# Five steps of a small side computation moved out of the first chunk of a gated layer into the last expert blocks, and two first products taken in two column parts

## The chip, the cores and the metric

The kernel runs on one core of a Trainium2 chip. The metric is the device time of one execution in microseconds (us). TensorE (PE) multiplies matrices, VectorE (DVE), ScalarE (ACT) and GpSimd (POOL) work on elements, and SyncE (SP) issues most transfers, in the order of its program. Each engine runs its own list of instructions in order and waits at an instruction until what it needs is there.

## The reference, cut to what matters

```python
def reference(q, k, v, modality_id, w_gate, modality_bias, w1, w2, w_in, w_out):
    x = windowed_attention(q, k, v)                  # 2304 tokens x 512
    logits = x @ w_gate + modality_bias[modality_id]
    e_idx = argmax(logits); gate = max(softmax(logits))   # one of 8 experts for each token
    for e in range(8):                               # the expert layer
        m = e_idx == e
        y[m] = gate[m] * (relu(x[m] @ w1[e]) @ w2[e])     # 512 -> 1024 -> 512
    h = y @ w_in                                     # the gated layer, 512 -> 2048 -> 512
    g = where(h >= 1, h, where(h <= -1, 0, (h + 1) ** 2 / 4))
    return g @ w_out
```

## The kernel before, in words

All products are made of parts in TensorE's fp32r form: an operand is split into a high part `h` and a low part `l` (a cast on ACT, then a subtraction on DVE or POOL), and three products h·h, h·l, l·h are added up. The kernel has three stages.

1. **Attention and routing.** Tokens are sorted by expert, in blocks of 128.
2. **Experts.** The loop over `u` (1 to 9) works on pairs of blocks, `b = 2u-1` and `b + 1`. `up_unit(x, q)` makes a quarter of the hidden layer (24 matmuls of 256 columns; four quarters, `q` 0 to 3), `relu` evicts it, and `down_unit(hh, i)` makes one block's output (24 matmuls of 512 columns). `put_y` scales the output and stores it to `ys` in DRAM. Half of an expert's weights (four tiles of 512 KB) is loaded into `RA` by `load_halves` at the start of the up half, the other half into `raw` at its end. Near the end the unused conversion space is given up (`half_ends(12)`), and the gated layer's weight groups `WG<-wis` are loaded into it.
3. **The gated layer.** Tokens come in three chunks `c` of 768, weights in groups `g` of 256 columns. A `unit` makes one group by a scheme with seven products (A11, A12, S1 to S4, A22) in place of eight, from sums and differences of the token blocks (`sum_x`, lines 1196) that are then split (`split_x`, lines 1189 and 1190). The products are accumulated in `mx`, `mz`, `mv`, `mw`. `also(k)` runs between the products and holds everything else, written out by hand: transposes of gathered tokens (`turn_y`, `typ`), loads and splits of later weight groups (`group_load`, `group_steps`), and the rests. When the chunk is done a second layer (`ob`) follows.

**The rests.** Each expert has a few tokens that fill no block. They are worked in small products, one expert `n` at a time, in steps `(n, k)`: k = 0 and 1 are `rest_up` (eight matmuls of 256 columns with 32 rows of weights, `rhp`), k = 2 turns the hidden rows (`rtp`), k = 3 and 4 are `rest_down` (four matmuls of 512 columns, `ryp`), k = 5, for odd `n` only, adds into `rsum`. The weights that a step k = 0, 1, 3 or 4 reads are four tiles of 256 KB (`WR`); there is one set of them, so the load for the next step is issued when the step's own matmuls have been issued and read them. `rest_end()` runs a step 0, 1, 3 or 4 and gives back its load, `rest_mid()` a step 2 or 5; each does nothing when the next step is not of its kind. The list of steps:

```python
rsteps = [(n, k) for n in range(UR) for k in range(6 if n % 2 else 5)]   # UR = 5
```

Before the change one `rest_end` runs at the end of each half pair `b` from 7 to 17, the others in the first chunk, one after each unit; the last one, (4, 4), in chunk 1. All engines but POOL run in the order in which the code is written (`manual_schedule`), POOL too in the gated layer.

Of the kernel before, what the change touches and what calls it, by code (L numbers as in the profile page):

```python
# [23 lines left out]
D = 512  # L24
# [16 lines left out]
TH = 384  # L41
# [44 lines left out]
def moe_kernel(tc, qh, kh, vh, wgh, mod, mbias, wall, winh, wouth, out):  # L86
    nc = tc.nc
    with ExitStack() as ctx:
# [218 lines left out]
                    yield  # L307

        def scaled(y, yp, k):
            nc.scalar.activation(y[:, :D], yp, AF.Copy, scale=k[:, 0:1])  # L310
            nc.scalar.copy(y[:, D:], k)

        def put_y(b, yp, tile=None):
            y = tile if tile is not None else mp.tile([P, XW], F32, name="y", bufs=2)
# [71 lines left out]
        def relu(hh, q, hp):  # L386
            h, l = (a[q].rearrange("p a t -> p (a t)") for a in hh)
            nc.scalar.activation(h, hp, AF.Relu)  # L388
            nc.vector.scalar_tensor_tensor(out=l, in0=hp, scalar=0.0, in1=h, op0=ALU.max, op1=ALU.subtract)  # L389

        def down_unit(hh, i):
            yp = bank("yp")
            for f in range(8):
                h, l = (a[f // 2][:, f % 2, i * P:i * P + P] for a in hh)
                wh, wl = (w[4 + f // 2][:, f % 2 * 512:f % 2 * 512 + 512] for w in (WH, WL))
                nc.tensor.matmul(yp, h, wh, start=f == 0, stop=False)  # L396
                nc.tensor.matmul(yp, h, wl, start=False, stop=False)
                nc.tensor.matmul(yp, l, wh, start=False, stop=f == 7)
            return yp
# [757 lines left out]
                return lambda: rest_load(*q) if q else None  # L1157
            return lambda: None

        RB0 = 7  # L1160

        def rests(b):

# [112 lines left out]
        with tc.manual_schedule(engines=ORDERED):  # L1276
# [63 lines left out]
            for u in range(1, UU):  # L1340
                b = 2 * u - 1
                last = u == UU - 1
                load_halves(2 * u)
                if u > 1 and not last:
                    for i in range(2):
                        xlast = xg_tile(2 * u + 1 + i)
                        gather(2 * u + 1 + i, xlast)
                if u > 1:
                    hh = h_tiles()
                    for q in range(4):  # L1350
                        relu(hh, q, up_unit(x, q))
                        if q == 1:
                            split_half(u, (4, 5))
                            rest_mid()
                        if q < 2 and (b, q) != (CVE, 0):
                            early(b)
                        if q == 2:
                            stores()
                            for v in units[b + 1]:
                                conv0(v)  # L1360
                    split_half(u, (6, 7))
                else:
                    for v in units[b + 1]:
                        conv0(v)
                if u == 1:
                    tokens(5, 9)
                done = convert(units[b])
                if u == 2:
                    tokens(13, UB + 2)
                if b == 13:  # L1370
                    order(mp.tile([P, XW], F32, name="y", bufs=2))
                rests(b)
                half_ends(b)
                b += 1
                if u > 1:
                    load_halves(2 * u + 1)
                if last:
                    wide = [new_raw("wide") for _ in range(4)]
                    for i in range(3):
                        fetch(i, wide[i][:, 0:XW])  # L1380
                if u == 1:
                    put_y(b - 1, down_unit(hh, 0))
                if not last:
                    for i in range(2):
                        turn_x(2 * u + 1 + i, x, i, new_gk())
                    split_half(u + 1, range(4))
                if u > 1:
                    put_y(b - 1, down_unit(hh, 0))
                    rest_mid()
                    early(b)  # L1390
                if last:
                    fetch(3, wide[3][:, 0:XW])
                    for i in range(3):
                        turn_y(i, ygs[i])
                    for o in ("A11", "A12"):
                        split_x(o)
                stores()
                for v in units[b + 1]:
                    conv0(v)
                if u == 1:  # L1400
                    tokens(9, 13)
                    idc = mp.tile([P, NE, NT], F32, name="idc")
                    nc.scalar.copy(idc, ids_ps)
                    mask = rest_tables()
                if u == 2:
                    rests_b(val, mask)
                put_y(b, down_unit(hh, 1))
                done = convert(units[b])
                if not last:
                    early(b)  # L1410
                    rests(b)
                half_ends(b)
                if u == UU - 2:
                    xgs, xs_u = {UB % 2: xg1, (UB + 1) % 2: xlast}, [gk[UB - 2], gk[UB - 1]]
                    yt = mp.tile([P, XW], F32, name="y", bufs=2)
                    gt = [new_gk() for i in range(2)]
                    more(UU)
# [12 lines left out]
                cfree.append(cfree[0])  # L1430
                return cfree.pop(0)

            def prod(o, s, out, first):
                h, l = (w[:, PROD[o]].rearrange("p (k w) -> p k w", k=2) for w in group_parts(None, s))
                xh, xl = sx[o]

                mms = [(w[:, k], xh[:, k]) for k in range(2) for w in (h, l)] + [(h[:, k], xl[:, k]) for k in range(2)]
                for n, (a, b) in enumerate(mms):
                    nc.tensor.matmul(out, a, b, start=first and n == 0, stop=n == 5, skip_group_check=not first)  # L1439

            def put_g(c, f, h, src):

# [17 lines left out]
            def unit(c, g, s, opened, also):  # L1460

                x, c1 = opened or open_x(s)
                also(0)
                z, v = bank("mz", (P, TH)), bank("mv", (P, TH))
                prod("S2", s, z, True)
                c2 = new_c()
                nc.vector.tensor_add(c2, z, c1)
                also(1)
                prod("S1", s, v, True)
                c5 = new_c()  # L1470
                nc.scalar.copy(c5, v)  # L1471
                also(2)
                if not opened:
                    close_x(c, g, s, x)
                also(3)
                prod("S3", s, z, False)
                nc.vector.tensor_add(c1, z, c1)
                also(4)
                prod("S4", s, v, False)
                nc.vector.tensor_add(c2, v, c2)  # L1480
                put_g(c, 2 * g, 1, c2)
                nc.vector.tensor_add(c5, c1, c5)  # L1482
                put_g(c, 2 * g + 1, 1, c5)
                also(5)
                w = bank("mw", (P, TH))
                prod("A22", s, w, True)
                nc.vector.tensor_add(c1, w, c1)
                put_g(c, 2 * g + 1, 0, c1)
                also(6)
# [83 lines left out]
            with tc.manual_schedule(engines=ORDERED | {E.Pool}):  # L1573
# [3 lines left out]
                for c in range(NCH):  # L1577
                    opened = {}
                    if c == 0:

                        for i in range(3):
                            opened[i] = open_x(ORD[0][i][1])
                            if i:
                                close_x(c, *ORD[0][i - 1], opened[i - 1][0])
                        turn_y(3, ygs[3])
                        close_x(c, *ORD[0][2], opened[2][0])
                        rest_mid()
                        load = rest_end()
                        turn_y(4, ygs[4])
                        for part, t in (((0, 256), 4), ((256, TH), 5)):  # L1590
                            if t > 4:
                                turn_y(t, ygs[t])
                            for i in range(2):
                                sum_x(i, nc.vector, part)
                            for o in ("S2", "S1"):
                                split_x(o, part)
                    for i, (g, s) in enumerate(ORD[c]):
                        last = i == NG - 1

                        def also(k):  # L1600
# [4 lines left out]
                                if k in (1, 2, 3):  # L1605
                                    split_x(("S3", "S4", "A22")[k - 1])
                            if c == 0:
                                if k == 3:
                                    rest_mid()
                                if k == 6 and i:  # L1610
                                    rest_end()()
                                if (i, k) == (0, 3):
                                    load()
                                for g, at in ((3, (0, 0)), (4, (0, 6)), (5, (1, 6)), (6, (2, 6))):
                                    if (i, k) == at:
                                        group_load(g, g)
                                if steps_at(1, 4, i, k):
                                    next(lg_)
# [140 lines left out]
```

## Time and profile before

| | |
|---|---|
| time, median of 3 runs | 808.7 us (808.5 to 810.07) |
| the profiled execution: its time | 812.92 us |
| its span in the trace | 811.2 us |
| TensorE busy in the span | 764.3 us, 94% |
| VectorE, ScalarE, GpSimd busy | 506.3, 349.5, 299.5 us |

The span is that of one profiled execution, from its first instruction to its last; the median is that of unprofiled runs. TensorE is busy nearly all the time; matmuls are pipelined, so a busy TensorE is not one at its peak.

### The profile page before, as it was taken

The page shows a single profiled execution, that of the slowest core. Times are in us where ns is not written, and L with a number is a line of the kernel's source. Part 1 is how long each engine was busy: PE and PEld are TensorE (multiplying, and loading weights), DVE is VectorE, ACT ScalarE, POOL GpSimd, SP SyncE. Part 2 cuts the span into 40 slices and gives each one's busy share as a digit, 9 for nine tenths or more (in the row PEclk, how much of TensorE's full clock was granted, in tenths as well). Part 3 has the DMA queues.
Part 4 walks back from the last instruction along what each step waited for, and adds up shares of the span by engine and source line. Part 5 has one row for each costly group of instructions (what it writes and reads, how often), then busy time and mean ns, then how long its engine had stood idle before and what let it go on. Part 6 is the DMA issues. An engine that isn't in the chain of part 4 may idle for free. (4 is left out here: it accounts for less than half of the span.)

```text
span 811.2 us, 14415 instructions
## 1 busy us (share of the span) xinstructions
PE 764.3 (94%) x4893; PEld 658.9 (81%) x4893; DVE 506.3 (62%) x1012; ACT 349.5 (43%) x827; POOL 299.5 (37%) x257
## 2 busy tenths in 40 slices
PE   7999779999999999898989888999999999999996
PEld 6888668999887887687778767999987788888884
DVE  6788888797775647412745644898878456553540
ACT  5899644233233226315333423343455435443340
POOL 5000562223332244111632321333744556475441
PEclk9999979999999999989899999999999999999999
DMA  9888942447797869234675554557855453343411
GB/s 206 232 232 251 290 122 50 147 169 253 244 329 256 285 224 375 87 117 151 204 245 167 182 205 149 188 186 230 271 207 149 121 150 116 105 130 102 138 53 39
DMA packets 101014, 149.21 MB, mean 184 GB/s; under 512 B 30096, under 2 KB 65456, under 8 KB 100928
## 3 DMA queue, kind: packets, MB, share of 16 engines
q1 hardware_dynamic: 95664, 132.30, 51.8%
q0 software_dynamic: 4736, 15.61, 6.1%
q8 instruction: 41, 0.67, 0.4%
q10 hardware_dynamic: 528, 0.26, 0.1%
q14 instruction: 45, 0.37, 0.1%
HBM read 132.00 MB, written 45.50 MB: 219 GB/s over the span
## 5 line engine op out<-in xcount | busy, mean ns | idle before, releaser
L1571 POOL TENSOR_TENSOR AR<-RA,AR 128x768 fp32r<-128x768 f32 x43 | 81.8, 1923 | 44.3 <-ACT AR L1570 44.2
L1683 PE MATMUL ob<-WG,AR 128*128 128x512 f32 x234 | 92.1, 394 | 1.2 <-POOL AR L1571 1.0
L82 POOL TENSOR_TENSOR cv_g<-cv_g,cv_a 128x512 f32<-128x512 f32 x32 | 45.2, 1426 | 129.5 <-DVE cv_a L80 98.2
L1681 PE MATMUL ob<-WG,AR 128*128 128x512 f32 x234 | 91.6, 391 | 0.0
L1682 PE MATMUL ob<-WG,AR 128*128 128x512 f32 x234 | 91.2, 390 | 0.0
L380 PE MATMUL hp<-xh,AR 128*128 128x256 f32 x512 | 73.5, 286 | 3.3 <-ACTq L1310 3.3
L380 PEld LDWEIGHTS hp<-xh,AR 128*128 128x128 f32 x512 | 66.6, 193 | 7.0 <-ACTq L1310 3.8
L1562 DVE TENSOR_SCALAR small<-RA 128x768 f32<-128x768 f32 x48 | 44.8, 935 | 36.7 <-DMA RA<-gs 36.7
L1563 ACT ACTIVATE small<-small,half 128x768 f32<-128x768 f32 x48 | 44.9, 937 | 41.5 <-DVE small L1562 41.5
L475 ACT ACTIVATE ex<-sm,nm 128x128 f32<-128x128 f32 x144 | 56.1, 394 | 15.2 <-DVE nm L468 14.8
L1439 PE MATMUL mz<-AR,WG 128*128 128x384 f32 x252 | 55.6, 357 | 6.7 <-ACT AR L1189 3.7
L1569 DVE TENSOR_TENSOR RA<-small,RA 128x768 f32<-128x768 f32 x48 | 56.0, 1167 | 6.3 <-ACT small L1563 5.2
L389 DVE SCALAR_TENSOR_TENSOR hl<-hp,hh 128x512 fp32r<-128x512 f32 x32 | 21.8, 689 | 53.9 <-ACT hh L388 33.5
L1439 PE MATMUL mv<-AR,WG 128*128 128x384 f32 x252 | 53.6, 347 | 1.5 <-ACT wide L1471 1.4
L1439 PEld LDWEIGHTS mz<-AR,WG 128*128 128x128 f32 x252 | 46.7, 199 | 9.8 <-ACT AR L1189 4.0
L1683 PEld LDWEIGHTS ob<-WG,AR 128*128 128x128 f32 x234 | 43.9, 188 | 13.2 <-POOL AR L1571 3.9
L1439 PE MATMUL mx<-AR,WG 128*128 128x384 f32 x252 | 52.5, 347 | 1.8 <-ACT small L1450 1.5
L1570 ACT CAST AR<-RA 128x768 fp32r<-128x768 f32 x48 | 39.9, 831 | 32.6 <-DVE RA L1569 15.8
L463 PE MATMUL sc<-K,qz 128*128 128x128 f32 x288 | 45.6, 309 | 8.3 <-DMA K<-in_kh_dram 5.0
L396 PE MATMUL yp<-AR,hh 128*128 128x512 f32 x128 | 51.6, 403 | 0.8 <-ACTq L351 0.8
L1439 PEld LDWEIGHTS mx<-AR,WG 128*128 128x128 f32 x252 | 45.2, 193 | 8.3 <-issue 6.4
L1682 PEld LDWEIGHTS ob<-WG,AR 128*128 128x128 f32 x234 | 43.9, 188 | 9.5
(395 smaller groups left out, 1734.4 us busy)
## 6 DMA issues: line engine op xcount, KB each, us to landing
WR<-in_wall_dram SPq DMA_DIRECT2D x80, 256.0 KB
RA<-in_wall_dram SPq DMA_DIRECT2D x36, 512.0 KB
raw<-in_wall_dram SPq DMA_DIRECT2D x36, 512.0 KB
RA<-gs SPq DMA_DIRECT2D x48, 384.0 KB
gs<-small SPq DMA_DIRECT2D x51, 192.0 KB
cv_r<-in_winh_dram SPq DMA_DIRECT2D x16, 512.0 KB
gs<-wide SPq DMA_DIRECT2D x36, 192.0 KB
V<-in_vh_dram SPq DMA_DIRECT2D x7, 768.0 KB
```

Of the source, the lines that this page charges most:

```text
L82: nc.gpsimd.tensor_add(z, z, x)
L380: nc.tensor.matmul(o, a, c, start=n == 0, stop=n == 11)
L396: nc.tensor.matmul(yp, h, wh, start=f == 0, stop=False)
L463: nc.tensor.matmul(sc[:, hp], Q[:, gi % 3, hp].rearrange("p a b -> p (a b)"), K[:, hp, s * 64:s * 64 + 128], start=True, stop=True)
L475: nc.scalar.activation(ex[:, hp], sm[:, hp], AF.Exp, bias=nm[:, hp:hp + 1], scale=1.0, accum_out=su[:, hp:hp + 1])
L1439: nc.tensor.matmul(out, a, b, start=first and n == 0, stop=n == 5, skip_group_check=not first)
L1563: nc.scalar.activation(GQ[n % 4], GQ[n % 4], AF.Square, scale=0.5, bias=half[:, 0:1])
L1569: nc.vector.tensor_max(GT[n % 5], GQ[n % 4], GT[n % 5])
L1571: eng.tensor_sub(l, GT[n % 5], h)
L1681: nc.tensor.matmul(obs[i], h[:, sl], wh, start=f == j == 0, stop=False)
L1682: nc.tensor.matmul(obs[i], h[:, sl], wl, start=False, stop=False)
L1683: nc.tensor.matmul(obs[i], l[:, sl], wh, start=False, stop=f == 7 and j == 1)
```

## The change

- In blocks 13 to 16 (`RX`) `rest_end` and `rest_mid` are called more often: after quarters 0, 1 and 2 of an up half, in the middle and at the end of the first `down_unit`. Nine steps, (1, 3) to (3, 1), run in these four blocks where four ran, and block 17 runs (3, 2) and (3, 3): (2, 4), (3, 0), (3, 1), (3, 2) and (3, 3) leave the gated layer. Chunk 0 keeps (3, 4), ahead of its units, and (3, 5) to (4, 3). The load for (4, 0) goes out in unit 3 in place of unit 4.
- In chunk 0 the transposes of the sixth token tile (`turn_y(5)`) are issued ahead of the splits of the first 256 columns, and unit 0's first products S2 and S1 are taken in two parts, 256 and 128 columns: S2 and S1 of the first part, then S2 and S1 of the second.
- `scaled` copies the gate columns ahead of the output, not behind it.

```diff
         def scaled(y, yp, k):
+            nc.scalar.copy(y[:, D:], k)
             nc.scalar.activation(y[:, :D], yp, AF.Copy, scale=k[:, 0:1])
-            nc.scalar.copy(y[:, D:], k)
...
-        def down_unit(hh, i):
+        def down_unit(hh, i, between=None):
             yp = bank("yp")
             for f in range(8):
+                if f == 4 and between:
+                    between()
...
-        RB0 = 7
+
+        RB0, RX = 7, (13, 14, 15, 16)
...
                         relu(hh, q, up_unit(x, q))
+                        if b in RX and q == 0:
+                            rest_mid()
                         if q == 1:
                             split_half(u, (4, 5))
+                            if b in RX:
+                                rest_end()()
+                            else:
+                                rest_mid()
+                        if b in RX and q == 2:
                             rest_mid()
...
-                    put_y(b - 1, down_unit(hh, 0))
-                    rest_mid()
+                    if b in RX:
+                        put_y(b - 1, down_unit(hh, 0, rest_mid))
+                        rest_end()()
+                    else:
+                        put_y(b - 1, down_unit(hh, 0))
+                        rest_mid()
...
-                put_y(b, down_unit(hh, 1))
+                if b in RX:
+                    put_y(b, down_unit(hh, 1, rest_mid))
+                else:
+                    put_y(b, down_unit(hh, 1))
...
-                prod("S2", s, z, True)
+                if (c, g) == (0, 0):
+                    prod("S2", s, z, True, PARTS[0])
+                    prod("S1", s, v, True, PARTS[0])
+                    prod("S2", s, z, False, PARTS[1])
+                else:
+                    prod("S2", s, z, True)
...
-                prod("S1", s, v, True)
+                if (c, g) == (0, 0):
+                    prod("S1", s, v, False, PARTS[1])
+                else:
+                    prod("S1", s, v, True)
...
-                        for part, t in (((0, 256), 4), ((256, TH), 5)):
-                            if t > 4:
-                                turn_y(t, ygs[t])
-                            for i in range(2):
-                                sum_x(i, nc.vector, part)
+                        for i in range(2):
+                            sum_x(i, nc.vector, PARTS[0])
+                        turn_y(5, ygs[5])
+                        for part in PARTS:
+                            if part[0]:
+                                for i in range(2):
+                                    sum_x(i, nc.vector, part)
                             for o in ("S2", "S1"):
                                 split_x(o, part)
...
-                                if k == 3:
+                                if k == 3 and i >= 4:
                                     rest_mid()
-                                if k == 6 and i:
+                                if k == 6 and i >= 5:
                                     rest_end()()
-                                if (i, k) == (0, 3):
+                                if (i, k) == (3, 3):
                                     load()
```

On TensorE, in the up half of block 13, the second to the fourth quarter and what follows stood so before (`hp` are the quarters, `rtp` and `ryp` are rest steps (1, 2) and (1, 3), `xp` the transposes of the next pair's tokens):

```order
L1087 MATMUL rtp<-ident,rh 128x128 x2
L380 MATMUL hp<-xh,AR 128x256 x8
L380 MATMUL hp<-xl,AR 128x256 x4
L380 MATMUL hp<-xh,AR 128x256 x8
L380 MATMUL hp<-xl,AR 128x256 x4
L380 MATMUL hp<-xh,AR 128x256 x8
L380 MATMUL hp<-xl,AR 128x256 x4
L380 MATMUL hp<-xh,AR 128x256 x8
L380 MATMUL hp<-xl,AR 128x256 x4
L351 UNCONDITIONAL_BRANCH
L1095 MATMUL ryp<-WR,rht 32x512 x4
```

After the change the same place has step (1, 3) after the second quarter and (1, 4) after the fourth:

```order
L1097 MATMUL ryp<-WR,rht 32x512
L351 UNCONDITIONAL_BRANCH
L1097 MATMUL ryp<-WR,rht 32x512 x3
L380 MATMUL hp<-xh,AR 128x256 x8
L380 MATMUL hp<-xl,AR 128x256 x4
L380 MATMUL hp<-xh,AR 128x256 x8
L380 MATMUL hp<-xl,AR 128x256 x4
L380 MATMUL hp<-xh,AR 128x256 x8
L380 MATMUL hp<-xl,AR 128x256 x4
L380 MATMUL hp<-xh,AR 128x256 x8
L380 MATMUL hp<-xl,AR 128x256 x4
L351 UNCONDITIONAL_BRANCH
```

The two rest steps of `down` now stand half an up half apart, where one stood; `L1097 MATMUL ryp<-WR,rht 32x512 x4`, step (1, 4), is the next row.

On SP this stood before the change behind the load for step (1, 4), of which the first row is the last of four tiles (`ISA` rows work out addresses; `er_i` and `on_i` are reads of registers):

```order
L1071 DMA WR<-in_wall_dram 128x512
L1225 DMA WG<-wis 128x1024
L1305 TENSOR_LOAD on_i
L1305 ISA x2
L241 ISA
L241 DMA raw<-in_wall_dram 128x1024
```

and this after it:

```order
L1073 DMA WR<-in_wall_dram 128x512
L1069 TENSOR_LOAD er_i
L1069 ISA x2
L1073 ISA
L1073 DMA WR<-in_wall_dram 128x512
L1073 ISA
L1073 DMA WR<-in_wall_dram 128x512
L1073 ISA
L1073 DMA WR<-in_wall_dram 128x512
L1073 ISA
L1073 DMA WR<-in_wall_dram 128x512
```

The load for (2, 0) now stands ahead of `WG<-wis` and `raw`. What stands ahead of the load for (1, 4) is as before: the load for (1, 3), the first `WG<-wis`, three register reads, four loads into `RA`.

On SP in chunk 0, around the load of the group that unit 7 works on (`WG<-wis`), there stood before:

```order
L1443 DMA gs<-small 128x384
L1067 TENSOR_LOAD er_i
L1067 ISA x2
L1071 ISA
L1071 DMA WR<-in_wall_dram 128x512
L1071 ISA
L1071 DMA WR<-in_wall_dram 128x512
L1071 ISA
L1071 DMA WR<-in_wall_dram 128x512
L1071 ISA
L1071 DMA WR<-in_wall_dram 128x512
L1225 DMA WG<-wis 128x1024
```

and now:

```order
L1464 DMA gs<-small 128x384 x3
L1464 DMA gs<-wide 128x384 x3
L1464 DMA gs<-small 128x384
L1228 DMA WG<-wis 128x1024
L1464 DMA gs<-small 128x384
```

The four loads `WR` for step (4, 0) no longer stand ahead of that `WG<-wis`; they stand seven stores (`gs`) earlier.

## Rows read from the trace of the kernel before

**Rows 1.** Page, part 1: busy us (share of the span) and instructions.

```profile
PE 764.3 (94%) x4893; PEld 658.9 (81%) x4893; DVE 506.3 (62%) x1012; ACT 349.5 (43%) x827; POOL 299.5 (37%) x257
```

**Rows 2.** Timeline of PE, blocks 13 to 16: start, us, instructions [idle before, releaser].

```profile
293.67 1.19 PE L380 MATMUL hp<-xh,AR 128*128 128x256 f32 x8
...
299.50 1.06 PE L1095 MATMUL ryp<-WR,rht 128*32 128x512 f32 x8
...
305.15 0.49 PE L396 MATMUL yp<-AR,hh 128*128 128x512 f32 x1 [0.77 <-ACTq L351]
...
314.36 1.06 PE L1095 MATMUL ryp<-WR,rht 128*32 128x512 f32 x8
...
327.70 1.07 PE L1080 MATMUL rhp<-WR,xst 128*32 128x256 f32 x16
...
340.93 1.07 PE L1080 MATMUL rhp<-WR,xst 128*32 128x256 f32 x16
```

**Rows 3.** Timeline of SP's queue, same blocks: when each load was issued.

```profile
288.35 3.10 SPq L1071 DMA_DIRECT2D WR<-in_wall_dram  x4
297.94 0.33 SPq L1225 DMA_DIRECT2D WG<-wis  x1
300.36 2.22 SPq L241 DMA_DIRECT2D RA<-in_wall_dram  x4
302.85 2.28 SPq L1071 DMA_DIRECT2D WR<-in_wall_dram  x4
```

**Rows 4.** Two stretches: busy time by engine, PE clock, DMA share, GB/s.

```profile
298.00:306.00 8.00, 6.88 (x43) 4.71 (x42) 2.81 (x6) 2.61 (x6) 2.14 (x2) 1.00 0.78 253
306.00:310.00 4.00, 4.00 (x17) 3.29 (x18) 3.56 (x9) 4.00 (x6) 0.70 (x2) 1.00 1.04 393
```

**Rows 5.** Timeline of PE in chunk 0, units 2 to 6.

```profile
408.21 1.06 PE L1080 MATMUL rhp<-WR,xst 128*32 128x256 f32 x12
411.59 0.63 PE L1080 MATMUL rhp<-WR,xst 128*32 128x256 f32 x4 [2.33 <-DMA WR<-in_wall_dram]
...
416.95 1.21 PE L1439 MATMUL mx<-AR,WG 128*128 128x384 f32 x6
...
421.90 1.06 PE L1095 MATMUL ryp<-WR,rht 128*32 128x512 f32 x8
...
426.15 1.20 PE L1439 MATMUL mx<-AR 128*128 128x384 f32 x6
...
429.72 1.21 PE L1439 MATMUL mw<-AR 128*128 128x384 f32 x6
...
440.67 1.79 PE L1080 MATMUL rhp<-WR,xst 128*32 128x256 f32 x16
...
447.31 1.32 PE L1439 MATMUL mx<-AR,WG 128*128 128x384 f32 x6 [1.52 <-ACT small L1450]
...
454.32 1.21 PE L1439 MATMUL mw<-AR,WG 128*128 128x384 f32 x6
```

**Rows 6.** Timeline of SP's queue in chunk 0.

```profile
403.19 2.06 SPq L1071 DMA_DIRECT2D WR<-in_wall_dram  x4
...
435.66 3.59 SPq L1071 DMA_DIRECT2D WR<-in_wall_dram  x4
439.30 0.43 SPq L1225 DMA_DIRECT2D WG<-wis  x1
```

**Rows 7.** Timeline of DVE in chunk 0: the first step on unit 7's weight group.

```profile
444.61 0.42 DVE L1234 TENSOR_TENSOR small<-WG 128x256 f32<-128x256 f32 x1 [5.81 <-DMA WG<-wis]
```

**Rows 8.** Timeline of all engines at unit 0's first products (S2 in mz, S1 in mv).

```profile
386.64 3.78 POOL L1196 TENSOR_TENSOR RA<-RA 128x768 f32<-128x768 f32 x2 [7.25 <-DVE RA L1196]
387.03 3.67 DVE L1190 TENSOR_TENSOR AR<-RA,AR 128x256 fp32r<-128x256 f32 x2 [0.47 <-ACT AR L1189]
387.05 2.75 PE L1439 MATMUL mz<-AR,WG 128*128 128x384 f32 x6 [3.74 <-ACT AR L1189]
...
391.56 1.46 PE L1439 MATMUL mz<-AR,WG 128*128 128x384 f32 x6
```

More of the change, by code (lines that the diff above doesn't have):

```diff
@@ L1431, in new_c, with prod @@
                 return cfree.pop(0)
-            def prod(o, s, out, first):
+            PARTS = ((0, 256), (256, TH))
+            def prod(o, s, out, first, part=ALLT):
                 h, l = (w[:, PROD[o]].rearrange("p (k w) -> p k w", k=2) for w in group_parts(None, s))
-                xh, xl = sx[o]
+                xh, xl = (x[:, :, part[0]:part[1]] for x in sx[o])
+                out = out[:, part[0]:part[1]]
                 mms = [(w[:, k], xh[:, k]) for k in range(2) for w in (h, l)] + [(h[:, k], xl[:, k]) for k in range(2)]
                 for n, (a, b) in enumerate(mms):
-                    nc.tensor.matmul(out, a, b, start=first and n == 0, stop=n == 5, skip_group_check=not first)
+                    nc.tensor.matmul(out, a, b, start=first and n == 0, stop=n == 5, skip_group_check=not first or part is not ALLT)
             def put_g(c, f, h, src):
```

## The prediction

> **What bounds the kernel now.** I read the page first: TensorE (PE) is busy for 94% of the span [rows 1], so time is won or lost where PE waits, or where it runs slowly behind a wait. Then I followed PE's timeline through the two stretches that the change touches, and at each wait the row of the queue that it waited for.
>
> In the expert blocks PE hardly waits. From the rest step at 299.50 us to the next at 314.36 it takes 14.86 us; the same work two blocks on, from 327.70 to 340.93, takes 13.23 [rows 2]. The excess of 1.63 lies at 305.15, where PE waits for ScalarE. In chunk 0 it waits more. Rest step (3, 1) starts at 408.21 and stops for 2.33 us for the last of its four weight tiles, issued from 403.19 on [rows 5, 6]. Around the change of unit at 440.67 there are waits again, for an evicted copy that ScalarE makes late [rows 5]. The row to see there is VectorE's: it had stood for 5.81 us, until 444.61, for the weights of unit 7 [rows 7], which SP had issued at 439.30, behind the four tiles of step (4, 0) [rows 6]; ScalarE's casts of these weights stand ahead of its evictions. The first stop of chunk 0 is 3.74 us at 387.05, for the split of S2 [rows 8].
>
> **What moving the steps costs in the expert blocks.** The steps' own work (some 1.0 us each, as the rows of 1.06 and 1.07 show, less the overlap with the next row) is the same on both sides: (2, 4), (3, 0), (3, 1), (3, 3) at 1.0 and two transposes, 4.1 us, leave chunk 0 and come in here. PE is full in both places, so it sums to nothing. What matters is that each step needs a load of four tiles (1.05 MB) that can start only when the step before is done, and that the steps now stand half an up or a down apart, 5.8 us (293.67 to 299.50 [rows 2]), where about 13 us lay between them.
>
> *Step (1, 3)* comes at 293.67 in place of 299.50. Its load was issued from 288.35 on [rows 3]. How long such a load takes, from its first issue to its last tile, the trace shows once: 403.19 to 411.59, 8.4 us, with other loads around it [rows 5, 6]. From below: issue 2.3 us, and 1.05 MB at 393 GB/s [rows 4] 2.7 us, together 5.0. So it lands between 293.4 and 296.8; the last tile is wanted at 294.4. A wait of 0 to 2.4 us; I take 1.4.
>
> *Step (1, 4)* is the dear one. Its load is issued right behind (1, 3), but on SP's queue it stands behind the first `WG<-wis` (0.5 MB), which went out only at 297.94 (the space that it fills is given up then), three register reads, and four loads into RA (2.1 MB) from 300.36 on; so it goes out from 302.85 on [rows 3], in the changed kernel as before, since nothing ahead of it has moved. PE is at the step at 293.67 + 1.0 + 1.4 + 5.8 = 301.9, before the load is even issued. When does it land? From 297.94 on 3.67 MB have to come in. At 253 GB/s until 306.00 and 393 after [rows 4] 2.02 MB are in by 306.00 and 3.59 by 310.00: the last tile lands at 310.2, and the step ends at 310.5. Without any wait it would end at 293.67 + 1.0 + 5.8 + 1.0 = 301.5. So **the two steps cost 9.0 us together**. From below: RA and this load, 3.15 MB, at 393 GB/s from 300.36 on, end at 308.4, 7.2 us. From above: 8.4 us from 302.85 on, 10.0 us. The Trainium skill, DMA: Bandwidth & Descriptors, section Queues, rings and completion order, says that descriptors of one issuing engine's queue are consumed in ring order on each DMA engine. No row here shows in which order the bytes of the two loads came; by that rule the tiles come after RA, as I summed, and without it the load could be in at 302.85 + 5.0 = 307.9 and the cost would be 6.7.
>
> *Behind the wait* PE's matmuls run slowly for a while. After the 2.33 us at (3, 1) that is measured: 408.21 to 416.95 is 8.74 us, and the same run of step, mx, mz, mv in a calm unit, 421.90 to 426.15, 4.25 [rows 5]. Of the 4.49 us lost 2.33 are the wait; **2.2 us** are the slow matmuls. I take that here too; the bounds are 0 and, the wait being much longer, 4.4.
>
> *Given back*: the excess of 1.63 us at 305.15 goes. ScalarE is ready at 305.2, when PE still stands at step (1, 4). **-1.6.**
>
> *The later steps* (2, 1), (2, 3), (2, 4) and (3, 1) have the step before them 5.8 + 1.0 = 6.8 us earlier. With a load time of 5.0 to 8.4 us the wait is 0 to 1.6 us each. I take **0.6** for all four, 6.4 as the upper bound. (2, 0) and (3, 0) stand a whole down and the transposes behind, and wait for nothing; (3, 3) has an up half.
>
> Sum here: 9.0 + 2.2 - 1.6 + 0.6 = **+10.2 us**.
>
> **What it gives in chunk 0.** Step (3, 1) is gone with its load: **-4.5** (the 4.49 above). Behind it unit 3 needs weight group 3, whose splits wait for nothing of the rests, so no other wait takes the place.
>
> Unit 7's weight group no longer stands behind the four tiles: SP can issue it behind the store of unit 4, at some 435.7 in place of 439.30 [rows 6], and the load has the queue to itself. It was in 5.3 us after its issue (439.30 to 444.61 [rows 6, 7]); it would be there by 441.0 at the latest, and by 439.4 at the bandwidth bound, where VectorE was ready at 444.61 - 5.81 = 438.8. So ScalarE's casts come 3.6 to 5.2 us earlier, and the evicted copy on which PE waited is in time. Step (4, 0) has its tiles too, since they are loaded a unit earlier. What PE loses there: 440.67 to 454.32 is 13.65 us, and the same run (step, mx, mz, mv, mx, mz, transposes, mv) in a calm unit, 421.90 to 429.72, 7.82 [rows 5]. **-5.8.** From below nothing, if the weights still come late.
>
> **The first products in two parts.** PE can begin S2 on 256 columns some 3 us earlier, but the end is set by the second part. VectorE's two subtractions for it took 3.67 us, from 387.03 to 390.70; GpSimd's two sums ran from 386.64 to 390.42 [rows 8]. VectorE's sums and subtractions of both parts stand in the same order as before, only the transposes move, so the last one will end at 390.7 again. What is left for PE then is two matmuls of 128 columns where it was two of 384: of the 0.86 us from 390.70 to 391.56 about two thirds go, **-0.6**. The twelve matmuls more lie in PE's wait; without that cover they would cost at most what twelve of 384 columns do, 2.4 us (six take 1.20 [rows 5]). The skill's page SBUF — State Buffer, section Who interferes with whom, says that a VectorE instruction with two SBUF inputs and a reading GpSimd instruction exclude each other for a whole instruction, and the first to start wins; [rows 8] agree, since a subtraction of 1.8 us comes out at half of GpSimd's time. By it the sum is the 0.6 above; without that lock the two subtractions would end by 388 and the gain would be near 3. `scaled` moves 0.2 us of ScalarE's work that nothing waits for: nothing.
>
> Sum: -4.5 - 5.8 - 0.6 = **-10.9 us**. Net 10.2 - 10.9 = **-0.7**. The profiled execution took 812.92 us, the median of the runs is 808.7, 0.5% less; a difference of this size is the same on either: 812.2 and **808.0 us**. A measurement of this kernel can tell 0.2%, 1.6 us, from no change. So I forecast no change that can be told: two large terms that nearly cancel.
>
> **Rivals.**
> *The later loads are late as well (slower).* Place: steps (2, 1) to (3, 1), four distances of 6.8 us. It decides once a load takes more than 6.8 us from its first issue. For it: the one load that the trace times took 8.4. Against: at the rate of [rows 4] a load that comes alone takes 5.0. At 1.6 each it is +5.8 on the forecast: 813.8.
> *The wait at (1, 4) is short and PE is not slowed behind it (faster).* 7.2 in place of 9.0, and 0 in place of 2.2: 804.0. For it: less competes with the load, since the next group and `raw` now stand behind it. Against: 3.15 MB don't come in faster than [rows 4] show.
> *VectorE gets its second part in ahead of GpSimd (faster).* Everything of the first unit moves up by 2.4 more: 805.6. Against: GpSimd waits for the same sum and needs no cast first.
> *The change doesn't do what it says in unit 5 (slower or the same).* Unit 7's group is late for another reason, as the stores ahead of it on SP wait for VectorE: only the slow step (4, 0), 0.7 of 5.8, is won: 813.1.
>
> **How the numbers follow.** Forecast 0.50, with its own range 805.5 to 810.0; the late loads 0.17; the short wait 0.15; VectorE first 0.08; unit 5 unmended 0.10. Of the forecast's half, 0.32 lie within 1.6 us of 808.7, 0.15 below, 0.03 above. Faster: 0.15 + 0.15 + 0.08 = 0.38; the same 0.32; slower: 0.03 + 0.17 + 0.10 = 0.30. The range leaves out the late loads and reaches from the short wait to unit 5: 803.5 to 813.2.
>
> **What the profile after would show.** Right: in block 13 a wait of PE for `WR` of 7 to 9 us ahead of the second `ryp`, slow matmuls behind it, and the end of block 16 some 14 us later than before; no wait at unit 2 or around unit 5 in chunk 0; S2 in two parts, the second ending with VectorE near GpSimd's second sum. Wrong: no such wait in block 13 (the change would be faster by some 10 us), or waits for `WR` at three or more of the later steps (slower), or unit 5 as before.

## The result, and the profile after

| | before | after |
|---|---|---|
| time, median of 9 runs each | 808.7 us (803.35 to 816.12) | 817.52 us (812.27 to 820.36) |
| the profiled execution: its time | 812.92 us | 817.52 us |
| its span | 811.2 us | 815.8 us |

The ratio of the runs is 1.0113, with an interval from 1.0081 to 1.0145: the change makes the kernel slower by 9 us, outside the range of the prediction. A second series of runs gave the same ratio (below). The two profiled executions differ by only 4.6 us, and that is what their rows can explain. The page of the changed kernel answers to [rows 1]:

```profile
span 815.8 us, 14439 instructions
PE 765.0 (94%) x4905; PEld 657.3 (81%) x4905; DVE 508.8 (62%) x1012; ACT 350.6 (43%) x827; POOL 300.8 (37%) x257
```

TensorE is busy as long as before, 765.0 us against 764.3; what is longer is its waiting. Its timeline in blocks 13 to 17 answers to [rows 2]:

```profile
286.74 1.07 PE L1082 MATMUL rhp<-WR,xst 128*32 128x256 f32 x16
293.80 3.52 PE L1097 MATMUL ryp<-WR,rht 128*32 128x512 f32 x8
...
309.39 3.83 PE L1097 MATMUL ryp<-WR,rht 128*32 128x512 f32 x8 [6.22 <-DMA WR<-in_wall_dram]
313.15 1.63 PE L293 MATMUL xp<-ident,xg 128*128 128x128 f32 x8
...
321.16 1.07 PE L1082 MATMUL rhp<-WR,xst 128*32 128x256 f32 x16
...
328.31 0.63 PE L1082 MATMUL rhp<-WR,xst 128*32 128x256 f32 x4 [0.28 <-DMA WR<-in_wall_dram]
...
329.62 1.26 PE L1082 MATMUL rhp<-WR,xst 128*32 128x256 f32 x12 [0.68 <-DMA WR<-in_wall_dram]
...
336.87 1.06 PE L1097 MATMUL ryp<-WR,rht 128*32 128x512 f32 x8
343.72 1.20 PE L1097 MATMUL ryp<-WR,rht 128*32 128x512 f32 x8
...
363.44 2.04 PE L380 MATMUL hp<-xh,AR 128*128 128x256 f32 x8 [3.88 <-PEq L1313]
```

Step (1, 3) at 293.80 takes 3.52 us where 1.06 is its work: its four tiles came one after another, the last weight load for it at 296.27. Step (1, 4) begins after a wait of 6.22 us, at 309.39, and takes 3.83. Step (2, 1) at 328.31 waits twice for a tile, 0.28 and 0.68. The last row, the first of block 17, stood in the kernel before at

```profile
345.34 2.07 PE L380 MATMUL hp<-xh,AR 128*128 128x256 f32 x8 [3.34 <-ACTq L1310]
```

so the blocks end 18.1 us later. SP's queue, as in [rows 3]:

```profile
297.58 0.33 SPq L1228 DMA_DIRECT2D WG<-wis  x1
300.01 2.23 SPq L241 DMA_DIRECT2D RA<-in_wall_dram  x4
302.49 11.09 SPq L1073 DMA_DIRECT2D WR<-in_wall_dram  x8
313.63 0.43 SPq L1228 DMA_DIRECT2D WG<-wis  x1
315.03 2.97 SPq L241 DMA_DIRECT2D raw<-in_wall_dram  x4
```

The load for (1, 4) goes out from 302.49, behind the first `WG` and the four loads into `RA`, as predicted. Eight `WR` stand in one row that lasts 11.09 us: the second four, for (2, 0), can't start until (1, 4) has read its tiles, so SP stands, and the next `WG` and `raw` behind it go out at 313.63 and 315.03. Four stretches, with the columns of [rows 4]:

```profile
298.00:306.00 8.00, 5.17 (x44) 4.96 (x43) 3.06 (x7) 2.12 (x4) 2.49 (x2) 1.00 0.82 265
306.00:314.00 8.00, 4.61 (x12) 1.58 (x13) 2.08 (x5) 0.00 (x0) 0.00 (x0) 0.59 0.70 252
314.00:322.00 8.00, 8.00 (x48) 5.74 (x46) 6.08 (x8) 5.84 (x9) 3.01 (x2) 0.98 0.94 314
322.00:330.00 8.00, 7.04 (x42) 4.73 (x36) 2.46 (x6) 1.55 (x4) 0.00 (x0) 1.00 0.87 341
```

The last two numbers are the DMA share and GB/s, the one ahead of them the granted clock: 0.59 from 306 to 314. In shorter stretches, while PE waits (302.5 to 309.39) the DMA engines are full, at a share of 1.01 and 375 GB/s. While (1, 4) runs (309.39 to 313.15) and the loads behind it are still held up on SP, the share is 0.34, 113 GB/s, and the granted clock is 0.50, the 1.2 GHz level, for all eight matmuls of the step.

In chunk 0 the waits of before at unit 2 and around unit 5 are gone, as predicted. The step at the change of unit, and the end of unit 5 (in [rows 5] 440.67 and 454.32):

```profile
450.17 1.07 PE L1082 MATMUL rhp<-WR,xst 128*32 128x256 f32 x16
457.96 1.21 PE L1460 MATMUL mw<-AR,WG 128*128 128x384 f32 x6
```

That is 7.79 us in place of 13.65; the calm unit of the prediction took 7.82. The products in two parts, as in [rows 8]:

```profile
402.93 1.58 PE L1460 MATMUL mz<-AR,WG 128*128 128x256 f32 x6 [1.25 <-ACT AR L1192]
...
407.29 0.44 PE L1460 MATMUL mz<-AR,WG 128*128 128x128 f32 x2 [0.70 <-DVE AR L1193]
...
409.25 0.44 PE L1460 MATMUL mv<-AR,WG 128*128 128x128 f32 x2 [1.08 <-DVE AR L1193]
409.81 2.21 PE L1460 MATMUL mz<-AR,WG 128*128 128x384 f32 x6
411.82 1.88 PE L1460 MATMUL mv<-AR,WG 128*128 128x384 f32 x6
```

Counted from the chunk's first matmul (391.68 after, 373.26 before), S2 begins 2.5 us earlier (11.25 in place of 13.79), but the next product, S3, only 0.17 (18.13 in place of 18.30), and unit 0's last product (`mw`) 0.6 later (21.86 in place of 21.26). VectorE's two subtractions for the second part still take as long as GpSimd's two sums beside them:

```profile
402.91 1.29 DVE L1193 TENSOR_TENSOR AR<-RA,AR 128x512 fp32r<-128x512 f32 x2 [0.70 <-ACT AR L1192]
...
405.47 3.73 DVE L1193 TENSOR_TENSOR AR<-RA,AR 128x256 fp32r<-128x256 f32 x2 [0.47 <-ACT AR L1192]
```

```profile
405.13 3.79 POOL L1199 TENSOR_TENSOR RA<-RA 128x768 f32<-128x768 f32 x2 [7.41 <-DMA WG<-wis]
```

The two for the first part, twice as wide, took 1.29 us with GpSimd idle; those for the second took 3.73. The Trainium skill, SBUF — State Buffer, section Who interferes with whom, has such a pair exclude each other; by that rule the second part could not come earlier, and the trace agrees. And S3 and S4 are now slow:

```profile
403.00:406.40 3.40, 3.40 (x16) 3.40 (x16) 2.90 (x5) 1.11 (x3) 1.27 (x1) 0.50 0.05 22
410.00:413.20 3.20, 3.20 (x11) 3.20 (x12) 2.76 (x4) 1.67 (x3) 2.28 (x4) 0.50 0.60 160
```

The granted clock is 0.50 in both stretches: once as S2's first part begins, and again, after PE's two short waits, under S3 and S4. In the profile of before one low stretch, from 385.3 to 392.1, lay under S2, S1 and the head of S3; S4 was out of it. Two stretches are not the rule: of the six profiles of this case that have the two parts, the other five show one, and it begins later or lasts longer than with whole products. What all six share is the clock over S3 and S4, 0.50 to 0.58, where the eight profiles with whole products have 0.68 to 1.00. S3 and S4 take 3.5 to 4.0 us in the six and 2.9 to 3.0 in the eight.

### The profile page after: what moved, and what is told of

The parts are those of the page before. It is cut to its first block, busy times and chain, and to the rows that moved or that the text cites. A ratio compares the mean times of both kernels' runs of the same rounds, so it can differ in the third digit from the quotient of the medians.

```text
span 815.8 us, 14439 instructions
## 1 busy us (share of the span) xinstructions
PE 765.0 (94%) x4905; PEld 657.3 (81%) x4905; DVE 508.8 (62%) x1012; ACT 350.6 (43%) x827; POOL 300.8 (37%) x257
## 5 line engine op out<-in xcount | busy, mean ns | idle before, releaser
L1713 PE MATMUL ob<-WG,AR 128*128 128x512 f32 x234 | 91.3, 390 | 0.0
L1460 PE MATMUL mz<-AR,WG 128*128 128x384 f32 (+2 forms) x258 | 54.7, 349 | 3.9 <-ACT AR L1192 1.3
L1460 PE MATMUL mv<-AR,WG 128*128 128x384 f32 (+2 forms) x258 | 53.8, 344 | 3.6 <-ACT wide L1500 2.1
L1714 PEld LDWEIGHTS ob<-WG,AR 128*128 128x128 f32 x234 | 43.9, 188 | 13.5 <-POOL AR L1600 4.2
L1599 ACT CAST AR<-RA 128x768 fp32r<-128x768 f32 x48 | 39.9, 830 | 32.3 <-PE ob L1713 16.2
L1713 PEld LDWEIGHTS ob<-WG,AR 128*128 128x128 f32 x234 | 43.9, 188 | 9.3
L1712 PEld LDWEIGHTS ob<-WG,AR 128*128 128x128 f32 x234 | 43.9, 188 | 9.1
L400 PE MATMUL yp<-AR,hl 128*128 128x512 f32 x128 | 50.6, 396 | 0.0
```

The lines of the kernel that those rows point to most:

```text
L1712: nc.tensor.matmul(obs[i], h[:, sl], wh, start=f == j == 0, stop=False)
L1713: nc.tensor.matmul(obs[i], h[:, sl], wl, start=False, stop=False)
L1714: nc.tensor.matmul(obs[i], l[:, sl], wh, start=False, stop=f == 7 and j == 1)
```

## The experiments

Theory A: the time is lost to the rests' weights, which can't come in as fast as the steps now ask for them in blocks 13 to 16. Theory B: it is lost to the first products in two parts. Ratios are to the kernel before, run on the same chip in the same series (its medians there: 807.42, 810.07 and 808.37 us).

**The two halves of the change, apart.** Moving the rests alone is the change without this part (and with the sums as before):

```diff
-                if (c, g) == (0, 0):
-                    prod("S2", s, z, True, PARTS[0])
-                    prod("S1", s, v, True, PARTS[0])
-                    prod("S2", s, z, False, PARTS[1])
-                else:
-                    prod("S2", s, z, True)
+                prod("S2", s, z, True)
...
```

> Only the rest steps and the copy in scaled are moved; the first products of chunk 0 and the order of turn_y(5) are as before the change. Theory A (the loss lies in waits of PE for the rests' weights in blocks 13 to 16): the time stays within 2 us of the changed kernel's, some 7 to 9 us over the kernel before, and block 17 starts 17 to 19 us later than before. Theory B (the products in two parts cost most of it, since their narrow matmuls and the waits between them leave the matmuls behind them slow): the time falls back to within 3 us of the kernel before.

Measured: 1.0055 (1.0026 to 1.0084), and in a later series, beside the kernel with whole products below, 1.0084 (1.0051 to 1.0117). That is 4.4 and 6.8 us over the kernel before; the first lies between what the two theories expect, the second near theory A. The place is theory A's: block 17 starts 17.8 us later, counted from step (1, 1).

> The kernel that moves the rests alone, again, beside the one above on the same chip. If its first ratio stands, 0.3 to 0.8% above the kernel before; if the difference to the changed kernel was chance, 0.9% or more.

The products in two parts alone, with the rests as before (`RX = ()` and the old slots in chunk 0):

> Only the first products in two parts, the order of turn_y(5) and the copy in scaled are changed; every rest step stands where it stood before. Theory A: within 1.5 us of the kernel before, since the part that ends last still waits for VectorE's second subtraction. Theory B: 5 us or more over the kernel before.

Measured: 1.0015 (0.9989 to 1.004), as theory A expects. So most of the loss is the rests', but the two do not quite add up to 1.13%. The changed kernel again, and the changed kernel with whole products but its new order of sums and transposes:

> The changed kernel again, nothing edited, beside the other kernels of this call, so that its ratio comes from more runs. If moving the rests and taking the products in two parts add up as the two kernels that did one part each (0.55% and 0.15%), it comes out near 0.7% above the kernel before, 813 us; if its first 1.13% stands, the two parts together cost more than apart.

> The changed kernel with the first products whole again; the sums and the transposes of token tile 5 stay in the changed order. The changed kernel is 1.13% above the kernel before, the one with the rests alone 0.55%. If it is the products in two parts that cost the other half per cent, this comes out near 0.55%, 4 us under the changed kernel. If it is the order of sums and transposes, or chance, it comes out nearer to 1.1%. In the trace the first unit, from its first product to its last, should take some 0.7 us less than the 21.9 of the changed kernel.

Measured: 1.0114 (1.006 to 1.0169), and 1.0087 (1.0055 to 1.012). The three series without the two parts lie at 0.55, 0.84 and 0.87%, the two with them at 1.13 and 1.14%. The intervals overlap, and 0.87% lies between the two values that were expected there. What the traces show is unit 0: from the chunk's first product to `mw` it takes 21.86 and 22.27 us with the parts, 21.24, 21.28 and 21.57 without. Over all the profiles of this case it is 21.47 to 22.27 with the parts (six, mean 21.9) and 21.22 to 21.57 without (eight, mean 21.3). So the two parts cost some 0.6 us there; for the other 2 us no row was found, and they may be chance.

**No loads.** The changed kernel without the loads that follow steps (1, 3) to (3, 0); these steps multiply what the tiles already hold; their own weights are left out. One of three such places:

```diff
-                                rest_end()()
+                                rest_end()(True)        # the step without its load
```

> The changed kernel without the seven loads that follow steps (1, 3) to (3, 0): those steps work on the weights that lie there already, so the rests' part of the output is left wrong, and nothing in blocks 13 to 16 waits for a load except step (1, 3). Theory A: block 17 starts only 5 to 8 us later than before (4.1 us of moved work and the wait of (1, 3)) and the time is 3 to 8 us under the kernel before. Theory B: the time stays over the kernel before.

Measured: 0.9949 (0.9926 to 0.9972), 802.76 us, 1.6% under the changed kernel: theory A. PE's timeline, steps (1, 4), (2, 0) and (2, 1):

```profile
302.20 1.07 PE L1099 MATMUL ryp<-WR,rht 128*32 128x512 f32 x8
...
311.04 1.07 PE L1084 MATMUL rhp<-WR,xst 128*32 128x256 f32 x16
317.84 1.07 PE L1084 MATMUL rhp<-WR,xst 128*32 128x256 f32 x16
```

No wait, each step 1.07. Block 17 starts 5.9 us later than before, counted from step (1, 1), and the time is 4.1 us under the kernel before; both were expected. The prediction's terms for chunk 0 alone, 10.9 us, would have given more. The edit takes away two things at once, the waits for the tiles and the hold-up of `WG` and `raw` on SP; no run separates them.

**The order on SP.** The loads into `RA` behind the load for (1, 4), not ahead of it:

```diff
-                load_halves(2 * u)
+                if b != RX[0]:
+                    load_halves(2 * u)
...
                             if b in RX:
                                 rest_end()()
+                                if b == RX[0]:
+                                    load_halves(2 * u)
```

> The changed kernel with one edit: in block 13 the four loads into RA for the next experts are issued on SP's queue behind the load of step (1,4), not ahead of it. Theory A1, the wait of 6.2 us at (1,4) comes from where its load stands on the queue: the load goes out at some 298 us, lands by 304.5, PE waits 0 to 2 us there, and the whole comes out 4 to 7 us under the changed kernel, at 810 to 813 us. Theory A2, the wait is the bytes' (everything that comes in from 297 on has to be in before PE can go on): PE waits as long, at the next converted weights in place of the step, and the time stays within 2 us of the changed kernel.

Measured: 1.0053 (1.002 to 1.0086), 813.07 us, half the loss gone, and 5 us under the changed kernel's median in the same series, 818.22: as far as the time goes, theory A1. On SP the order is turned round:

```profile
296.48 2.07 SPq L1073 DMA_DIRECT2D WR<-in_wall_dram  x4
300.03 2.23 SPq L241 DMA_DIRECT2D RA<-in_wall_dram  x4
```

and PE's timeline shows both theories at work:

```profile
300.79 3.21 PE L1097 MATMUL ryp<-WR,rht 128*32 128x512 f32 x8
...
311.41 1.80 PE L1082 MATMUL rhp<-WR,xst 128*32 128x256 f32 x16
321.59 0.63 PE L1082 MATMUL rhp<-WR,xst 128*32 128x256 f32 x4 [2.59 <-DMA WR<-in_wall_dram]
...
322.89 1.70 PE L1082 MATMUL rhp<-WR,xst 128*32 128x256 f32 x12 [0.67 <-DMA WR<-in_wall_dram]
```

Step (1, 4) begins at 300.79, 4.3 us after its load's first issue; behind `RA` it was 6.9 (302.49 to 309.39). It still takes 3.21 us, since its tiles come one after another, the last weight load at 302.96. The Trainium skill, DMA: Bandwidth & Descriptors, section Queues, rings and completion order, has one engine's descriptors consumed in the order of its ring; by that rule a load waits for the bytes ahead of it, and the trace agrees. But then a wait comes back at (2, 1), 2.59 and 0.67 us. Its load goes out from 312.83 on, when the DMA engines are full:

```profile
306.00:314.00 8.00, 7.97 (x42) 4.94 (x41) 6.73 (x10) 5.66 (x9) 3.84 (x2) 1.00 1.03 397
314.00:322.00 8.00, 5.41 (x26) 3.84 (x24) 1.52 (x4) 0.69 (x1) 0.00 (x0) 1.00 1.03 398
```

They move 397 and 398 GB/s at a share of 1.03. Step by step, as start of the step's first matmul counted from that of (1, 1), in us:

| | no loads | changed | `RA` behind |
|---|---|---|---|
| (1, 4) | 16.2 | 22.7 | 16.3 |
| (2, 0) | 25.1 | 34.4 | 26.9 |
| (2, 1) | 31.9 | 41.6 | 37.1 |
| (2, 3) | 38.9 | 50.1 | 47.0 |
| (3, 1) | 60.2 | 71.5 | 68.3 |
| chunk 0's first product | 91.3 | 104.9 | 102.1 |

The 6.4 us won at (1, 4), 7.5 at (2, 0), are 3.1 by (2, 3).

**Later blocks.** Three steps, (2, 4) to (3, 1), moved to blocks 15 to 17, where for the most part less comes in (the DMA share is 0.4 to 0.7 from 322 to 370 us, against 1.02 to 1.03 from 306 to 322):

```diff
-        RB0, RX = 7, (13, 14, 15, 16)
+        RB0, RX = 7, (15, 16, 17)
...
-                                if k == 6 and i >= 5:
+                                if k == 6 and i in (3, 5, 6, 7):
                                     rest_end()()
-                                if (i, k) == (3, 3):
+                                if (i, k) == (0, 3):
                                     load()
```

> The changed kernel with the extra rest steps in blocks 15, 16 and 17 in place of 13 to 16, so that no two steps stand closer than a quarter pair while the big weight loads are queued; chunk 0 runs (3, 3) ahead of its units and (3, 4) to (4, 3) after units 3, 5, 6 and 7. Theory A: no wait of PE for the rests' weights above 2.5 us in the expert blocks, and the time is 6 to 10 us under the kernel before, since chunk 0 keeps its gain. Theory B: the time is at or above the kernel before, as in the changed kernel.

> The kernel that moved three steps to blocks 15 to 17, now without the products in two parts. If the two parts cost what the kernel with them alone showed (0.15%), it comes out 1 us under that kernel, near 0.4% under the kernel before, 804.5 us. If they cost nothing, the same 0.23% under.

Measured: 0.9977 (0.9953 to 1.0001) with the products in two parts, 0.9961 (0.9927 to 0.9994) without, so 1.3 us between them, as expected, though within the intervals. Theory A was half right: no wait for the rests' weights in the expert blocks is above 2.5 us (the longest is 1.09, at (2, 0)), but the time was expected 6 to 10 us under the kernel before. From (1, 1) to chunk 0's first product it is 92.5 and 91.1 us, against 104.9 in the changed kernel and 86.5 in the one before; three steps are 3.1 us of work, so away from blocks 13 and 14 they cost 1.5 to 3 us beyond it, where four cost 14.

**Unit 7's weights without any move.** The kernel before, with one issue put ahead of another on SP at the end of unit 4:

```diff
-                                if k == 6 and i:
+                                if k == 6 and i and i != 4:
                                     rest_end()()
...
                                 group_load((7, 0, 7)[c], 0)
+                                if c == 0:
+                                    rest_end()()
```

> The kernel before with one edit: in the first chunk the weight group of unit 7 is issued on SP ahead of the four tiles of step (4,0), not behind them; no step is moved. If the 5.8 us that PE loses around unit 5 come from the late group alone, the group is in by 441 us, VectorE doesn't stand, PE loses 1 to 2 us at step (4,0), whose tiles now come 0.5 to 1.5 us later, and the whole comes out 4 to 5 us under the kernel before, 803 us. If the loss is the step's and its load's, whatever the order, it stays within 1.5 us of the kernel before.

Measured: 0.9925 (0.9893 to 0.9956), 804.56 us. SP's queue, then VectorE's first step on the weights, then PE at step (4, 0):

```profile
434.72 0.44 SPq L1225 DMA_DIRECT2D WG<-wis  x1
436.26 2.12 SPq L1071 DMA_DIRECT2D WR<-in_wall_dram  x4
```

```profile
439.12 0.96 DVE L1234 TENSOR_TENSOR small<-WG 128x256 f32<-128x256 f32 x1 [0.38 <-DMA WG<-wis]
```

```profile
441.15 0.63 PE L1080 MATMUL rhp<-WR,xst 128*32 128x256 f32 x4 [0.48 <-DMA WR<-in_wall_dram]
...
442.55 1.19 PE L1080 MATMUL rhp<-WR,xst 128*32 128x256 f32 x12 [0.77 <-DMA WR<-in_wall_dram]
```

VectorE stands for 0.38 us where it stood for 5.81 [rows 7]; PE waits 0.48 and 0.77 us for the tiles, which now come second. So VectorE's wait came from the order of the two loads, and two exchanged issues mend it. What that is worth is known less well: by the runs 3.6 to 8.7 us, and by the profiles chunk 0 takes 88.6 us from its first product to chunk 1's, where the two profiles of the kernel before have 92.4 and 90.8 (below).

**Step (3, 0) a unit earlier**, in that kernel, to give (3, 1)'s load more time (`i not in (1, 4)` in place of `i and i != 4`):

> The kernel before with unit 7's weight group ahead of the tiles of step (4,0), and with step (3,0) a unit earlier, behind unit 0 in place of unit 1, so that the load of step (3,1) goes out 6 us earlier. If the wait at (3,1) comes from the 7 us between the two steps, it goes, with the slow matmuls behind it: 4 us more under the kernel before than the 0.75% of the reordering alone, 800 us. If the load takes longer where it now is, beside weight group 4, or (3,0) itself waits for its tiles, it gives 0 to 2 us.

Measured: 0.992 (0.9886 to 0.9953), 802.94 us: nothing that can be told from the 0.9925 above. In its timeline (of an execution of 810.6 us, 7.7 over the median of its runs), steps (3, 1) and (3, 3):

```profile
411.98 1.07 PE L1080 MATMUL rhp<-WR,xst 128*32 128x256 f32 x16
...
425.18 1.21 PE L1095 MATMUL ryp<-WR,rht 128*32 128x512 f32 x2 [2.95 <-DMA WR<-in_wall_dram]
```

The wait at (3, 1) is gone, and (3, 3) waits 2.95 us in its place.

**The kernel before again:**

> The kernel before once more, unedited, for a second profile of it and for the size of a difference that means nothing. Ratio within 0.3% of 1. If the profile shown of before was a slow draw, this one comes out some 3 to 5 us under its 812.92 us.

Measured: 0.9998 (0.9967 to 1.0029). Its profiled execution took 808.43 us, 4.5 less than the one shown of before. At the change to unit 5 VectorE stands nearly as long, but PE loses less:

```profile
442.21 0.42 DVE L1234 TENSOR_TENSOR small<-WG 128x256 f32<-128x256 f32 x1 [5.06 <-DMA WG<-wis]
```

```profile
439.01 1.98 PE L1080 MATMUL rhp<-WR,xst 128*32 128x256 f32 x16
...
451.80 1.28 PE L1080 MATMUL rhp<-WR,xst 128*32 128x256 f32 x12 [1.36 <-DMA WR<-in_wall_dram]
```

From step (4, 0) to the end of unit 5 (`mw` at 448.68) it is 9.67 us there, not 13.65; the next step, (4, 1), then waits 1.36 us. All of chunk 0, from its first product to chunk 1's, took 92.4 us in the first profile of before and 90.8 in this one.

## Why the prediction was wrong

The mechanisms were the right ones: a long wait at (1, 4), whose load stands behind `RA` on SP; no more waits at unit 2 and around unit 5; products in two parts that VectorE and GpSimd hold up. What failed is the sum of sizes, since the forecast was a small difference of two large terms. Most of it is the term for blocks 13 to 16, 4 us too small. The rest is a gain in chunk 0 about 1 us too large and a loss in unit 0 where a gain was forecast; some 3 to 4 us of the 9 have no row.

- **Blocks 13 to 16: +10.2 forecast, +14.3 measured.** Chunk 0's first product comes 18.4 us later, of which 4.1 are moved work. (Counted from step (1, 1), the five profiles with these moves and their order of loads have 104.2 us on average, the five of kernels whose rests stand as before 85.6: +14.5.) This is the step that failed most. *(1, 3)*: 1.4 taken, with 0 to 2.4 as bounds; 3.52 - 1.06, 2.5 us. *(1, 4) with the slow matmuls behind it*: 7.6 + 2.2 taken; by the table it costs 9.4 up to (2, 0), against the kernel without loads. That was right, but not as I split it: the step ended at 313.15, where I had 310.5, and the slow matmuls were for the most part its own, at a granted clock of 0.50. *Later steps*: 0.6 taken for four; (2, 1) alone, with what follows up to (2, 3), costs 1.8 more, the other three nothing. The last 2.3 us, for which the sum had no term, lie between (3, 1) and the gated layer, where the granted clock is 0.57 from 362 to 370; the other four profiles that the average above is of lose 0.4 to 2.1 there, so it is chance in part. *Given back*: the kernel without loads comes out 0.8 us over the kernel before from (1, 1) to chunk 0, moved work taken off, with the wait at (1, 3) still in it, so the 1.6 us were won.
- **Chunk 0's waits: -10.3 forecast.** The delay of 18.4 us at its first product is 19.0 behind unit 0 and 5.0 at the first product of chunk 1, so 14.0 are won, 4.1 of them moved work: 9.9. But that profile had lost more there than another of the same kernel did (92.4 and 90.8 us), so in the mean it is nearer to 9. The prediction has unit 7's group in by 439.4 at the bandwidth bound; its rows give some 437.0 (0.5 MB at 393 GB/s from 435.7), and nothing hangs on it. With the two issues exchanged the group was in 4.4 us after its issue (434.72 to 439.12).
- **Products in two parts: -0.6 forecast, +0.6 measured.** S3 did begin 0.17 us earlier, but S3 and S4 ran at the low clock, as they do in all six profiles with the parts, and took 3.7 us in place of 3.0. I had priced the twelve more matmuls as hidden by the wait, and not asked what the clock does when one long wait becomes three short ones.
- **From the profile to the median.** I carried a difference within one profiled execution over to the median. By the profiled executions the change costs 4.6 us, where -0.7 was forecast; by the runs it is 9.1. The profile shown of before lay 4.2 us over its median, the one of after on it. Segment by segment, the five profiles with the moves (two of the changed kernel, three with whole products) take 104.2 us on average from (1, 1) to chunk 0 and 79.2 in chunk 0; the two profiles of before 86.5 and 91.6. Together that is 17.7 - 12.4 = +5.3, which fits the rests alone (0.55 and 0.84%, 4.4 and 6.8 us). Behind chunk 0 the moved kernels are not slower (343.3 to 345.2 us to the end, 345.6 and 345.0 before). For the changed kernel, at 9.1, some 3 to 4 us stay open.
- **The rivals.** *Later loads late*: true at (2, 1), not at the other three. *Short wait*: no, though the order of two loads would have made it so at the first place. *VectorE first* and *unit 5 unmended*: no.

## What to carry to other kernels

A load that a moved step needs is part of the move: the steps had 13 us between them, and a load took 6.5 to 8.8 us from its first issue to its last tile (296.48 to 302.96 ahead of the experts' weights, 302.49 to 311.31 behind them). Where the DMA engines were full, at a share of 1.03, half of what was won at one step, (1, 4), was lost again by (2, 3). Before work is moved to get a load out of the way, try to issue the load that is waited for first: in chunk 0 that gave 6 us (3.6 to 8.7) and needed no move, where the best kernel with moved steps gave 0.4%, 3 us; the intervals of the two overlap.

When a forecast is a difference of two terms of 10 us, each known to 30%, its range is theirs, and a single profile adds some us of its own.

## What the runs showed that was not expected

- Two profiled executions of one kernel differ by 4.5 us (812.92 and 808.43), and the same wait of VectorE, 5.81 and 5.06 us, cost PE 5.8 us in one and 1.9 in the other within unit 5, with 1.36 of wait in the next.
- Taking two products in two parts each, with short waits of PE between them, went in all six profiles with a granted clock of 0.50 to 0.58 over the two products behind them, S3 and S4, which themselves waited for at most 0.12 us. Once it was two low stretches within 11 us, else one that came later or lasted longer than the one with whole products. No run separates the waits from the narrower matmuls as its cause.
